# Attention and a two-layer feed-forward block on one core: three pairs of feature tiles, DVE transposes placed behind the low parts, and a first chunk in a written order with its masks put into PSUM by TensorE

## The chip, the cores and the metric

The kernel runs on one core of a Trainium2 chip. The metric is device time in microseconds (us) of one execution, lower is better; the value that counts is the median of the runs shown. Engines are called TensorE (PE, with its weight loads PEld), VectorE (DVE), ScalarE (ACT), GpSimd (POOL) and SyncE (SP, which issues most DMAs).

## The reference

Eight batches, eight heads, 576 positions, head size 64. Heads 0 to 3 see the last 32 positions, heads 4 to 7 see every 32nd position up to their own. Then comes a feed-forward block with a squared ReLU.

```python
def _attn_ref(q, k, v):
    scores = scale * np.matmul(q, k.transpose(0, 1, 3, 2))
    rel = pos[:, None] - pos[None, :]
    mask_local = (rel >= 0) & (rel < stride)                       # stride = 32, heads 0..3
    mask_strided = (rel >= 0) & (pos[None, :] % stride == pos[:, None] % stride)   # heads 4..7
    scores = np.where(masks[None], scores, -1000000000.0)
    attn = np.exp(scores - np.max(scores, axis=-1, keepdims=True))
    attn = attn / (np.sum(attn, axis=-1, keepdims=True) + 1e-09)
    return np.matmul(attn, v)
...
x = attn_out.transpose(0, 2, 1, 3).reshape(B * S, H * D)           # 4608 x 512
h = np.maximum(x @ w_in, 0.0)                                      # w_in 512 x 2048
return (h * h) @ w_out                                             # w_out 2048 x 512
```

## The kernel before

The 4608 tokens are cut into nine chunks of 512 (`NCHUNK`). A chunk is 16 rows of 32 positions (`RUNS` lists from which batches; a run is a stretch of rows of one batch). For each chunk the attention output is made as a transposed tile x, in two halves: `"l"` for the local heads and `"s"` for the strided heads. Each half stands as a high part (`xlh`, `xsh`, a rounded float32r copy) and a low part (`xll`, `xsl`, the rest), so that three float32r products (high x high, high x low, low x high) stand for one float32 product.

The feed-forward block has 16 feature tiles of 128. `up(c, j)` makes tile j of chunk c with 12 products of 512 columns in a PSUM bank (bank j % 2). ACT then takes relu and square and casts the result to `gh` (L411 to L413; in chunk 0 ACT and DVE share this, L408 and L409), and DVE subtracts to get the low part `gl` (L414), which reads the bank of `up` for the last time. `gh` and `gl` come from `gpool` with two buffers each. `down(c, js)` adds tile by tile into four PSUM banks of y, 12 products for a tile (L429), two tiles at a time from chunk 1 on. The order on TensorE from chunk 1 on is: up j, up j+1, down j-2 and j-1, up j+2, and so on.

The attention of chunk c+1 is worked in beside chunk c. `local(c)` is a generator: loads; scores (L232) and mask add (L184); maximum, subtraction and exponential; sum and division; 16 transposes of 32 x 256 on DVE (L263), four at a step; outputs (L278) with copy and low part of x (L285, L286). `take` runs the next step where `plan` or, for chunk 0, `plan0` says, behind the last TensorE instruction. `strided(c)` is a generator too: GpSimd multiplies (L353, L375) and DVE reduces (L354, L376), with loads `qs`, `ks`, `vs` from a pool `s3` of five slots, and ends with x written by ACT and GpSimd (L387, L388). `xpool` has two buffers, so the x of chunk c+1 can be written when chunk c-1 has been used.

The weights come as raw 64-bit numbers. `convert()` makes a high and a low float32 part of each of the 16 weight blocks, in two pieces of 512 columns: ACT scales the raw block (L128) and makes `z` (L143), DVE joins `z` to the word (L146), ACT or DVE makes the high part (L150, L152), GpSimd the low part (L153). In the start `z` stands in PSUM banks 0 and 1, the same as those of `up`. `behind` lets these steps follow an instruction of the last `up`.

Chunk 0 starts with 60 products of zeros, the local scores and, in `strided0()`, the strided scores of rows 0 to 7 of two batches, done by TensorE with 32 x 32 blocks: 128 float32 products, which show as 256 instructions (L322).

Within a program the framework places each engine's instructions in an order that a planner works out ahead of time from estimated durations, earlier traced instructions first; `issue_after(i)` sets an edge on `i`'s own engine: what is traced under it stands behind `i` there. On the chip each engine works through its list in order.

Of the kernel before, what the change touches and what calls it, by code (L numbers as in the profile page):

```python
# [18 lines left out]
STR = 32  # L19
# [3 lines left out]
P = 128  # L23
# [20 lines left out]
NWARM = 60  # L44
NEARLY = 3
# [23 lines left out]
def attn_moe(ctx: ExitStack, tc, qk_d, v_d, qk_p, v_p, q_s, k_s, v_s, w_in, w_out, masks, consts, out):  # L69
# [5 lines left out]
    gpool = pool("gpool", 2)  # L75
# [17 lines left out]
    warm = const.tile([P, P // 2], F32, name="warm")  # L93
    nc.gpsimd.memset(warm, 0.0)
    zero = warm.bitcast(BF16)

    last = {}
# [6 lines left out]
    zhome, zturn = (0, 1), iter(range(1000))  # L104

    def fetch(k):

        p, which = order[k]
        src = (w_out if which else w_in)[p].bitcast(U32).rearrange("p (n t) -> p n t", t=2)
        if k < 12:  # L110
            raw = wpool.tile([P, 1024, 2], U32, name=f"raw{k}", tag=f"w{k + 8 if k < 8 else k + 4}")
            nc.sync.dma_start(out=raw, in_=src)
            raws[k] = [(raw, slice(0, 1024))]
        else:
            raws[k] = []
            for i in range(0, 1024, WP):
                raw = spool.tile([P, WP, 2], U32, name=f"raw{k}_{i}", tag="s3", bufs=5)
                nc.sync.dma_start(out=raw, in_=src[:, i : i + WP])
                raws[k].append((raw, slice(i, i + WP)))

    def convert():

        split = None

        def scale(k):
            for raw, _ in raws[k]:

                nc.scalar.activation(f32(raw[:, :, 1]), f32(raw[:, :, 1]), AF.Prelu, scale=2.0**-112, alpha=-(2.0**32))  # L128

        scale(0)  # L130
        for k in range(NFT):
            p, which = order[k]
            t = wpool.tile([P, 2, 1024], F32R, name=f"w{which}_{p}", tag=f"w{k}")
            (wo if which else wi)[p] = t[:, 0], t[:, 1]
            cuts = [(raw[:, i : i + WP], sl.start + i) for raw, sl in raws.pop(k) for i in range(0, sl.stop - sl.start, WP)]
            for raw, at in cuts:

                if zhome is None:
                    z = ypool.tile([P, WP], F32, name=f"z{k}_{at}", tag="ysb").bitcast(U32)
                else:  # L140
                    z = psum(zhome[next(zturn) % len(zhome)], f"z{k}_{at}").bitcast(U32)
                w, hi, lo = raw[:, :, 1], t[:, 0, at : at + WP], t[:, 1, at : at + WP]
                first_step = nc.scalar.activation(z, raw[:, :, 0], AF.Copy, bias=-0.49, scale=2.0**-29 * (1 - 2.0**-9))  # L143
                if split:
                    split()
                last["v"] = nc.vector.scalar_tensor_tensor(out=w, in0=w, scalar=3, in1=z, op0=ALU.logical_shift_left, op1=ALU.bitwise_or)  # L146

                def split(w=w, hi=hi, lo=lo, at=at, k=k):
                    if k == 0 or at:
                        last["v"] = nc.vector.tensor_copy(hi, f32(w))  # L150
                    else:
                        last["a"] = nc.scalar.copy(hi, f32(w))  # L152
                    last["g"] = nc.gpsimd.tensor_sub(lo, f32(w), f32(hi))  # L153
                    if at and 4 <= k < 12:
                        fetch(k + 4)

                if k == 0 and at:
                    split()
                    split = None
                if not at and k + 1 < NFT and k + 1 in raws:  # L160
                    with tc.issue_after(first_step.ins):
                        scale(k + 1)
                yield
        split()
# [12 lines left out]
    def softmax(u, s, e, mask, n, first):  # L177

        sv = [t[:, : 8 * n].rearrange("p (g w k) -> p g w k", g=2, w=4) for t in s]
        mx = small.tile([P, 16], F32, name=f"mx{u}", tag="lmx")  # L180
        sm = small.tile([P, 16], F32, name=f"sm{u}", tag="lsm")
        halves = [slice(8 * h, 8 * (h + 1)) for h in range(2)]
        for h, sl in enumerate(halves):
            nc.vector.tensor_tensor(out=e[:, sl].rearrange("p (g w) k -> p g w k", g=2), in0=sv[h], in1=mask, op=ALU.add)  # L184
        yield
        wide = lambda t, sl: t[:, sl].unsqueeze(2).broadcast_to([P, 8, n])
        if first:
            parts = halves
        else:
            parts = [slice(0, 16)]  # L190
            wide = lambda t, sl: t.unsqueeze(2).broadcast_to([P, 16, n])
        for sl in parts:
            nc.vector.tensor_reduce(out=mx[:, sl], in_=e[:, sl], op=ALU.max, axis=AX.X)
        for h, sl in enumerate(parts):
            eng = nc.vector if first and not h else nc.gpsimd
            eng.tensor_sub(e[:, sl], e[:, sl], wide(mx, sl))
        for h, sl in enumerate(parts):
            last["a"] = nc.scalar.activation(e[:, sl], e[:, sl], AF.Exp, scale=SCALE)
            last[f"exp{h}"] = last["a"]
        yield  # L200
        for h, sl in enumerate(parts):
            nc.vector.tensor_reduce(out=sm[:, sl], in_=e[:, sl], op=ALU.add, axis=AX.X)
            nc.vector.tensor_scalar_add(sm[:, sl], sm[:, sl], 1e-9)
            nc.vector.reciprocal(sm[:, sl], sm[:, sl])
            if first and h:
                last["g"] = nc.gpsimd.tensor_mul(e[:, sl], e[:, sl], wide(sm, sl))
            else:
                last["v"] = nc.vector.tensor_mul(e[:, sl], e[:, sl], wide(sm, sl))
        yield

    def local(c):

        first = c == 0
# [6 lines left out]
        mk = mpool.tile([P, 4, 2 * STR], F32, name=f"mk{c}", tag="mk")  # L220
        (nc.scalar if first else nc.sync).dma_start(out=mk, in_=masks[c])
        yield
        rows = rows_of(c)
        s = [psum(3 + h, f"s{c}_{h}") for h in range(2)]
        for w in range(4):
            for pr in range(2):
                for b in range(4):
                    r = 4 * w + b
                    k0 = TC + rows[r][2]
                    for h in range(2):  # L230
                        hd = slice(D * h, D * (h + 1))
                        last["mm"] = nc.tensor.matmul(  # L232
                            s[h][STR * b : STR * (b + 1), (4 * pr + w) * 64 : (4 * pr + w + 1) * 64],
                            qk[pr][hd, STR * r : STR * (r + 1)], qk[pr][hd, k0 : k0 + 64], start=True, stop=True,
                        )
        e = lpool.tile([P, 16, 2 * STR], F32, name=f"e{c}", tag="e")
        yield from softmax(f"{c}", s, e, mk.unsqueeze(1).broadcast_to([P, 2, 4, 2 * STR]), 2 * STR, first)
        if first:
            vt = wpool.tile([P, 2, 1024], F32, name="v0", tag="w6")
# [437 lines left out]
```

## Time and profile before

| | us |
|---|---|
| median of 3 runs | 967.02 |
| lowest, highest | 966.3, 973.57 |
| the profiled execution, in all | 965.91 |
| its span, first to last instruction | 964.1 |
| TensorE busy (matmul) in the span | 871.2 |
| DVE, ACT, GpSimd busy | 544.0, 331.0, 511.3 |
| mean granted TensorE clock | 0.95 of full speed |

A profiled execution is read on its own time: the span is its length from the first to the last instruction, and 1.8 us of the measured time lie around it. A granted clock of 1.00 is TensorE at 2.4 GHz, 0.5 is 1.2 GHz, and a mean between them is a mix in time. "Releaser" is the instruction whose end let a waiting one go; "issue" is idle time for which the profile shows no cause.

### The profile page before, as it was taken

The numbers are of one execution on the slowest core, as the hardware profiler recorded it, in microseconds if no ns is written. First come the engines' busy times: TensorE is split into PE (matmuls) and PEld (weight loads), VectorE is DVE, ScalarE is ACT, GpSimd is POOL, SyncE is SP. The second block draws the span as 40 slices with busy tenths as digits, with TensorE's granted clock in tenths as the row PEclk, the third lists the DMA queues.
The fourth block names the chain that finished last, engine by engine and source line by source line (L and its number), as shares of the span: only waits on it lengthen the run. The fifth ranks groups of instructions, "written<-read, shape, count | busy, mean of one in ns | idle before, by whom it ended". The sixth has DMA issues, their size and how long they took to land. (4 is left out here: it accounts for less than half of the span.)

```text
span 964.1 us, 15516 instructions
## 1 busy us (share of the span) xinstructions
PE 871.2 (90%) x6252; PEld 710.8 (74%) x6252; DVE 544.0 (56%) x1047; ACT 331.0 (34%) x574; POOL 511.3 (53%) x532
## 2 busy tenths in 40 slices
PE   5399888997999989997989897998889998999997
PEld 5377667786878777786778785876678886888886
DVE  4498867765686558755776567554866152111111
ACT  3365643332333233332323232332223332333332
POOL 2484477486767868558768494767767100000000
PEclk9599899999999989998989998998989999999999
DMA  9625143222120222022300430121300120001001
GB/s 379 283 96 184 36 137 121 85 85 96 51 71 30 97 67 94 0 66 94 114 28 1 134 115 11 41 82 64 113 1 1 48 88 1 1 1 44 0 1 44
DMA packets 23096, 72.39 MB, mean 75 GB/s; under 512 B 2544, under 2 KB 4848, under 8 KB 21488
## 3 DMA queue, kind: packets, MB, share of 16 engines
q1 hardware_dynamic: 22592, 71.05, 21.2%
q8 instruction: 49, 0.80, 0.3%
q10 hardware_dynamic: 432, 0.34, 0.1%
q14 instruction: 23, 0.19, 0.1%
HBM read 61.95 MB, written 9.44 MB: 74 GB/s over the span
## 5 line engine op out<-in xcount | busy, mean ns | idle before, releaser
L429 PE MATMUL y<-w,gh 128*128 128x512 f32 x1152 | 354.9, 390 | 0.0
L402 PE MATMUL h<-xlh,w 128*128 128x512 f32 x576 | 217.8, 420 | 67.9 <-DVE gl L414 61.2
L353 POOL TENSOR_TENSOR pq<-ks,qs 128x512 f32<-128x512 f32 (+2 forms) x224 | 216.5, 994 | 81.8 <-DMA ks<-k_s 44.4
L375 POOL TENSOR_TENSOR pp<-vs,sc 128x320 f32<-128x320 f32 (+11 forms) x224 | 208.5, 967 | 95.6 <-issue 65.9
L429 PEld LDWEIGHTS y<-w,gh 128*128 128x128 f32 x1152 | 216.5, 188 | 45.2
L429 PE MATMUL y<-w,gl 128*128 128x512 f32 x576 | 223.2, 389 | 0.0
L402 PE MATMUL h<-xsh,w 128*128 128x512 f32 x576 | 208.7, 404 | 0.0
L414 DVE TENSOR_TENSOR gl<-h,gh 128x512 fp32r<-128x512 f32 x144 | 98.9, 686 | 175.8 <-ACT gh L413 174.7
L402 PEld LDWEIGHTS h<-xlh,w 128*128 128x128 f32 x576 | 115.3, 200 | 104.3 <-DVE gl L414 72.9
L354 DVE TENSOR_REDUCE sc<-pq 128x8 f32<-128x512 f32 (+2 forms) x224 | 116.0, 534 | 108.7 <-POOL pq L353 107.3
L411 ACT ACTIVATE h<-h 128x512 f32<-128x512 f32 x128 | 74.5, 582 | 290.5 <-PE h L402 286.3
L413 ACT CAST gh<-h 128x512 fp32r<-128x512 f32 x144 | 84.5, 588 | 210.9 <-PE y L429 190.4
L376 DVE TENSOR_REDUCE qs<-pp 128x64 f32<-128x64 f32 (+12 forms) x224 | 117.9, 533 | 62.4 <-POOL pp L375 61.3
L402 PEld LDWEIGHTS h<-xsh,w 128*128 128x128 f32 x576 | 114.1, 198 | 25.2
L429 PEld LDWEIGHTS y<-w,gl 128*128 128x128 f32 x576 | 108.1, 188 | 22.6
L402 PE MATMUL h<-xll,w 128*128 128x512 f32 x288 | 118.4, 412 | 0.0
L402 PE MATMUL h<-xsl,w 128*128 128x512 f32 x288 | 116.0, 404 | 0.0
L412 ACT ACTIVATE h<-h 128x512 f32<-128x512 f32 x128 | 74.5, 582 | 3.7
L402 PEld LDWEIGHTS h<-xsl,w 128*128 128x128 f32 x288 | 57.1, 198 | 12.7
L402 PEld LDWEIGHTS h<-xll,w 128*128 128x128 f32 x288 | 57.8, 201 | 10.9
L153 POOL TENSOR_TENSOR w<-raw,w 128x512 fp32r<-128x512 f32 x32 | 44.9, 1407 | 36.5 <-ACT w L152 19.5
L263 DVE STREAM_TRANSPOSE pt<-e 32x256 f32<-32x256 f32 x128 | 55.7, 435 | 1.8
(67 smaller groups left out, 429.8 us busy)
## 6 DMA issues: line engine op xcount, KB each, us to landing
vs<-v_s SPq DMA_DIRECT2D x18, 576.0 KB, 4.3
y<-ysb SPq DMA_DIRECT2D x35, 256.0 KB, 2.6
v<-v_d SPq DMA_DIRECT2D x16, 512.0 KB, 4.9
qk<-qk_d SPq DMA_DIRECT2D x14, 544.0 KB, 5.1
raw<-w_in SPq DMA_DIRECT2D x7, 1024.0 KB, 11.2
raw<-w_out SPq DMA_DIRECT2D x5, 1024.0 KB, 13.3
ks<-k_s SPq DMA_DIRECT2D x8, 576.0 KB, 4.3
raw<-w_out SPq DMA_DIRECT2D x6, 512.0 KB, 5.3
```

The costliest lines, as they stand in the source:

```text
L153: last["g"] = nc.gpsimd.tensor_sub(lo, f32(w), f32(hi))
L263: nc.vector.transpose(out=pt[to : to + STR, :, STR * b : STR * (b + 1)], in_=e5[STR * b : STR * (b + 1), :, a, STR * half : STR * (half + 1)],
L353: nc.gpsimd.tensor_mul(pv, kt[:, a : a + m, :], qt[:, i - i0 : i - i0 + 1, :].broadcast_to([P, m, D]))
L354: nc.vector.tensor_reduce(out=sc[:, i - i0, a : a + m], in_=pv, op=ALU.add, axis=AX.X)
L375: nc.gpsimd.tensor_mul(pv, vt[:, a : a + nd, :n], sc[:, il : il + 1, :n].broadcast_to([P, nd, n]))
L376: nc.vector.tensor_reduce(out=ot[:, il, a : a + nd], in_=pv, op=ALU.add, axis=AX.X)
L402: done = nc.tensor.matmul(ph, wi[p][a][:, wsl], x["ls"[kt // 2], b][:, kt % 2, :], start=n == 0, stop=n == 11)
L411: nc.scalar.activation(ph, ph, AF.Relu)
L412: nc.scalar.activation(ph, ph, AF.Square)
L413: last["gh"] = nc.scalar.copy(gh, ph)
L414: nc.vector.tensor_sub(gl, ph, f32(gh))
L429: done = nc.tensor.matmul(y_ps[c][t], gg[:, sl], w[:, wsl], start=j == 0 and k == 0, stop=j == NFT - 1 and k == 2)
```

## The change

- `gpool` gets three buffers instead of two: three pairs of `gh` and `gl`.
- `take` places the steps of `local` also behind the last low part `gl` on DVE, the transposes in groups of four to a step among them.
- `up` sorts its 12 products by half and part of x, and becomes a generator that pauses after the fourth product. In chunk 0 the first four tiles use banks 0, 1, 3 and 4.
- The strided part gets two slots for queries of its own (`sq`) and three slots (`s3`) for keys and values instead of five for all; in chunks 1 to 3 keys and values come in one load (`kv_s`). In chunk 0 the strided steps of chunk 1 stand behind the last `gl` on DVE and the last weight step on GpSimd.
- Chunk 0 up to its second `up` is a function `begin()`, whose instructions keep the written order on each engine (`in_order`). The masks go into PSUM by products of the identity with the mask, and the scores are added to them; maximum and subtraction read PSUM. The strided weights are put into zero-padded 128 x 128 blocks, so that the strided outputs are 32 products of 128 columns (before: 128 of 32). Fetches of raw weights 1 to 3 are made to wait for instructions of other engines. Only the first weight piece has its `z` in PSUM.
- The raw weights 12 to 14 also come whole, and only the last one in two pieces through `s3`.

The diff, cut to its core:

```diff
-    gpool = pool("gpool", 2)
+    gpool = pool("gpool", 3)
...
+    @contextmanager
+    def in_order():
+        traced = nc.cur_bb.bb.instructions
+        n = len(traced)
+        yield
+        for i in traced[n:]:
+            if i.engine in ends:
+                tc.add_manual_dep(i, ends[i.engine].name, mybir.DependencyInfo(mybir.DependencyClass.NoSync, mybir.DependencyReason.DATA), reason="in order")
+            ends[i.engine] = i
+
+    def wait(ins, after):
+        tc.add_manual_dep(ins.ins, after.ins.name, mybir.DependencyInfo(mybir.DependencyClass.Sync, mybir.DependencyReason.DATA), reason="gate")
...
-        if k < 12:
-            raw = wpool.tile([P, 1024, 2], U32, name=f"raw{k}", tag=f"w{k + 8 if k < 8 else k + 4}")
+        if k < 15:
+            raw = wpool.tile([P, 1024, 2], U32, name=f"raw{k}", tag=f"w{RAW[k]}")
...
+    def piece(k, raw, at, t, home=None):
+        z = psum(home, f"z{k}_{at}") if home is not None else ypool.tile([P, WP], F32, name=f"z{k}_{at}", tag="ysb")
...
+    def begin():
+        zero = lpool.tile([P, 256], F32, name="zero", tag="e")
+        nc.vector.memset(zero, 0.0)
...
+        zeros(12)
+        qk = loads(0)
...
+        fetch(0)
...
+        for h in range(2):
+            for pr in range(2):
+                nc.tensor.matmul(s[h][:, 256 * pr : 256 * (pr + 1)], ident, mk.rearrange("p w k -> p (w k)"), start=pr == 0, stop=False, skip_group_check=True)
+        scores(0, qk, s, False)
+        ss = [ybank(f"ss{h}") for h in range(2)]
+        for h in range(2):
+            nc.tensor.matmul(ss[h][:, :256].rearrange("p (n k) -> p n k", k=STR), ident, mask_s.unsqueeze(1).broadcast_to([P, 8, STR]), start=True, stop=False, skip_group_check=True)
...
+        scale(0)
+        ka, kb = (piece(*c, home=h) for c, h in zip(cuts(0), (0, None)))
+        next(ka)
+        for h in range(2):
+            top = nc.vector.tensor_reduce(out=st["mx"][:, half[h]], in_=sv[h], op=ALU.max, axis=AX.X)
+        for h in range(2):
+            nc.vector.tensor_sub(el[:, half[h]], sv[h], wide(st["mx"][:, half[h]], 2 * STR))
+            nc.scalar.activation(el[:, half[h]], el[:, half[h]], AF.Exp, scale=SCALE)
+        wait(fetch(1), top)
...
+        wait(fetch(2), nc.scalar.activation(es, es, AF.Exp, scale=SCALE))
...
+        wait(zeros(14), top)
...
+        pts = wpool.tile([P, 16, P], F32, name="pts0", tag="w5")
+        nc.gpsimd.memset(pts, 0.0)
+        x = x_tiles(0)
+        o = [psum(3 + a, f"o0_{a}") for a in range(2)]
+        outputs([vt[:, pr] for pr in range(2)], pt, o)
+        xs = [by_parity(x, o, a) for a in range(2)]
+        for src, (xh, _) in xs:
+            done = nc.scalar.copy(xh, src)
+        nc.vector.tensor_mul(es, es, wide(st["sms"], STR))
+        for b in range(4):
+            blk = slice(STR * b, STR * (b + 1))
+            nc.vector.transpose(out=pts[blk, :, blk], in_=es[blk])
...
+        ups = [up(0, j) for j in range(2)]
+        for u in ups:
+            next(u)
+        wait(fetch(3), done)
+        for k in range(4, 8):
+            last["f"] = fetch(k)
...
-                    for b in range(4):
-                        ks = slice(STR * b, STR * (b + 1))
-                        last["mm"] = nc.tensor.matmul(
-                            o[b][STR * hd : STR * (hd + 1), (a * 4 + w) * STR : (a * 4 + w + 1) * STR],
-                            v4[ks, n, STR * a : STR * (a + 1)], pts[ks, n], start=True, stop=True,
-                        )
...
+                    nc.tensor.matmul(o[a][STR * hd : STR * (hd + 1), P * w : P * (w + 1)], v4[:, n, STR * a : STR * (a + 1)], pts[:, n], start=True, stop=True)
...
-            qt = spool.tile([P, MI, D], F32, name=f"qs{u}", tag="s3", bufs=5)
-            kt = spool.tile([P, NI, D], F32, name=f"ks{u}", tag="s3", bufs=5)
-            vt = spool.tile([P, D, NI], F32, name=f"vs{u}", tag="s3", bufs=5)
+            qt = spool.tile([P, MI, D], F32, name=f"qs{u}", tag="sq", bufs=2)
             nc.sync.dma_start(out=qt[:, :ni], in_=q_s[b, :, i0:i1])
+            if i1 == S0:
+                kv = spool.tile([P, 2, S0 * D], F32, name=f"kv{u}", tag="s3", bufs=3)
+                nc.sync.dma_start(out=kv, in_=kv_s[b])
...
+            else:
+                kt = spool.tile([P, NI, D], F32, name=f"ks{u}", tag="s3", bufs=3)
+                vt = spool.tile([P, D, NI], F32, name=f"vs{u}", tag="s3", bufs=3)
...
-        ph = psum(j % 2, f"h{c}_{j}")
-        prods = [(kt, a, b) for kt in range(4) for a, b in ((0, "h"), (0, "l"), (1, "h"))]
-        if c == 0 and j < 2:
-            prods.sort(key=lambda t: (t[1], t[0] // 2, t[2]))
+        ph = psum((0, 1, 3, 4)[j] if c == 0 and j < 4 else j % 2, f"h{c}_{j}")
+        prods = [(k, a, b) for k in range(4) for a, b in ((0, "h"), (1, "h"), (0, "l"))]
+        prods.sort(key=lambda t: (t[0] // 2, t[2]) if c else (t[0] // 2, t[2], t[1]))
...
-                    for i in (last["pe"], *(weights_end.values() if c == 2 else ())):
+                    for i in (last["pe"], last["gl"], *(weights_end.values() if c == 2 else ())):
...
-                if c == 1:
-                    st = behind(weights_end, st)
+                if c < 2:
+                    st = behind(weights_end if c else {"v": last["gl"], "g": last["g"]}, st)
...
+    for s in range(NS + 2):
+        with tc.issue_after(last["f"].ins):
+            slot(s)
```

## Rows read from the trace of the kernel before

**Rows 1.** Stretches: us, busy PE, PEld, DVE, ACT, POOL, mean granted clock, DMA, GB/s.

```profile
0.00:55.00 55.00, 29.14 (x773) 25.80 (x774) 28.25 (x58) 18.18 (x30) 21.64 (x29) 0.72 0.72 291
55.00:150.00 95.00, 84.80 (x591) 68.39 (x590) 79.30 (x123) 53.57 (x89) 58.29 (x52) 0.95 0.39 127
150.00:866.00 716.00, 664.78 (x4483) 540.41 (x4483) 421.65 (x846) 228.60 (x404) 431.34 (x453) 0.96 0.18 59
866.00:964.00 98.00, 92.47 (x408) 76.22 (x407) 14.76 (x22) 30.61 (x53) 0.00 (x0) 1.00 0.06 22
```

**Rows 2.** Waits of TensorE, whole span: who for whom, us, times, longest.

```profile
PE h L402 <- DVE gl L414: 61.2, 22, 5.8
PE os L322 <- issue: 8.4, 2, 4.4
```

**Rows 3.** The same waits, from 150 to 866 us.

```profile
PE h L402 <- DVE gl L414: 51.0, 18, 5.8
```

**Rows 4.** Chain of waits near the end: start, length, what.

```profile
847.44 2.00 PE o L278 x128
...
882.31 5.44 PE y L429 x24
887.75 5.44 PE h L402 x24
```

**Rows 5.** Timeline of TensorE at the scores taken in chunk 7.

```profile
780.43 1.48 PE L232 MATMUL s<-qk 64*32 64x64 f32 x128
```

**Rows 6.** Timeline of ACT and DVE in the last chunk: square, cast, low part.

```profile
880.24 0.58 ACT L412 ACTIVATE h<-h 128x512 f32<-128x512 f32 x1
...
884.84 0.59 ACT L413 CAST gh<-h 128x512 fp32r<-128x512 f32 x1 [1.30 <-PE y L429]
885.46 0.69 DVE L414 TENSOR_TENSOR gl<-h,gh 128x512 fp32r<-128x512 f32 x1 [7.42 <-ACT gh L413]
```

**Rows 7.** Timeline around the wait for the low part of tile 12, chunk 1.

```profile
231.14 1.57 POOL L353 TENSOR_TENSOR pq<-ks,qs 128x512 f32<-128x512 f32 x2 [3.50 <-DMA ks<-k_s]
...
231.77 0.59 ACT L413 CAST gh<-h 128x512 fp32r<-128x512 f32 x1 [1.65 <-PE y L429]
...
238.68 1.10 DVE L354 TENSOR_REDUCE sc<-pq 128x8 f32<-128x512 f32 x2 [1.11 <-POOL pq L353]
239.70 0.68 DVE L414 TENSOR_TENSOR gl<-h,gh 128x512 fp32r<-128x512 f32 x1
240.44 0.79 PE L402 MATMUL h<-xlh,w 128*128 128x512 f32 x1 [5.75 <-DVE gl L414]
```

**Rows 8.** Timeline around a wait for the low part of tile 3, chunk 4.

```profile
481.86 6.71 DVE L263 STREAM_TRANSPOSE pt<-e 32x256 f32<-32x256 f32 x15
488.61 0.69 DVE L414 TENSOR_TENSOR gl<-h,gh 128x512 fp32r<-128x512 f32 x1
489.35 0.80 PE L402 MATMUL h<-xlh,w 128*128 128x512 f32 x1 [2.75 <-DVE gl L414]
```

**Rows 9.** Timeline of GpSimd: first steps of the strided parts of chunks 5 and 8.

```profile
322.86 0.16 POOL L345 MEMSET sc<- 128x72 f32 x1
...
639.39 0.19 POOL L345 MEMSET sc<- 128x108 f32 x1
```

**Rows 10.** Timeline of TensorE in the start of chunk 0.

```profile
24.62 3.66 PE L278 MATMUL o<-pt,v 64*64 64x32 f32 x124 [0.81 <-DVE pt L255]
...
33.65 1.54 PE L322 MATMUL os<-tmp_s 32*32 32x32 f32 x128 [4.03 <-issue]
...
46.43 1.22 PE L402 MATMUL h<-xlh,w 128*128 128x512 f32 x2 [6.50 <-DVE raw L146]
```

**Rows 11.** Groups of DVE by line, 0 to 46 us: busy, mean ns, idle before.

```profile
L146 DVE SCALAR_TENSOR_TENSOR raw<-raw,z 128x512 uint32<-128x512 uint32 x5 | 3.4, 681 | 0.4 <-ACT z L143 0.4
```

**Rows 12.** The same, 55 to 150 us.

```profile
L146 DVE SCALAR_TENSOR_TENSOR raw<-raw,z 128x512 uint32<-128x512 uint32 x26 | 26.5, 1030 | 6.1 <-ACT z L143 5.9
```

**Rows 13.** DMA issues of the page: count, KB each, median us to landing.

```profile
vs<-v_s SPq DMA_DIRECT2D x18, 576.0 KB, 4.3
```

More of the change, by code (lines that the diff above doesn't have):

```diff
@@ L121, in convert @@
-    def convert():
[L123 to L159, printed above, removed]
@@ new lines, in scale, with cuts @@
+    def scale(k):
+        for raw, _ in raws[k]:
+            nc.scalar.activation(f32(raw[:, :, 1]), f32(raw[:, :, 1]), AF.Prelu, scale=2.0**-112, alpha=-(2.0**32))
+    def cuts(k):
+        p, which = order[k]
+        t = wpool.tile([P, 2, 1024], F32R, name=f"w{which}_{p}", tag=f"w{HOME[k]}")
+        (wo if which else wi)[p] = t[:, 0], t[:, 1]
+        return [(k, raw[:, i : i + WP], sl.start + i, t) for raw, sl in raws.pop(k) for i in range(0, sl.stop - sl.start, WP)]
+    def convert():
+        before = None
+        for k in range(3, NFT):
+            for k, raw, at, t in cuts(k):
+                g = piece(k, raw, at, t)
+                step = next(g)
+                if before:
+                    run(before)
+                    if at == 0 and k - 1 in NEXT:
+                        fetch(NEXT[k - 1])
+                next(g)
+                before = g
@@ L160, in convert @@
                 if not at and k + 1 < NFT and k + 1 in raws:
-                    with tc.issue_after(first_step.ins):
+                    with tc.issue_after(step.ins):
                         scale(k + 1)
                 yield
-        split()
+        run(before)
     xt = {}
@@ L214, in local, with loads @@
+    def loads(c):
         nk = STR * (CR + len(RUNS[c]))
@@ L219, in local, with scores @@
             qk.append(t)
-        mk = mpool.tile([P, 4, 2 * STR], F32, name=f"mk{c}", tag="mk")
-        (nc.scalar if first else nc.sync).dma_start(out=mk, in_=masks[c])
-        yield
+        return qk
+    def scores(c, qk, s, start):
         rows = rows_of(c)
-        s = [psum(3 + h, f"s{c}_{h}") for h in range(2)]
         for w in range(4):
@@ L316, in strided0 @@
+        next(ka)
+        next(kb)
+        scale(2)
+        v4 = vs.rearrange("p (n d) -> p n d", d=D)
+        o = [ybank(f"os{a}") for a in range(2)]
         for a in range(2):
@@ L523, in attn_moe @@
-    next(st)
-    for k in range(NEARLY, 8):
-        fetch(k)
-    with tc.issue_after(last["pe"].ins):
-        last["pe"] = zeros(0, 40, exp_l)
-    with tc.issue_after(last["pe"].ins):
-        next(lo)
-    next(st)
-    for _ in range(2):
-        next(ungated)
-    chain(lo)
-    chain(st)
-    weights = behind({"a": last["a"]}, ungated)
-    for _ in range(2 * NEARLY - 2):
-        next(weights)
-    zhome = None
+    plan0 = (2, 4, 6, 7, 8, 9, 10, 11, 13)
+    with in_order():
+        done, ups = begin()
@@ L540, in attn_moe, with slot @@
+    for u in ups:
+        run(u)
+    ungated = convert()
+    weights_end = st = cost = ds = None
+    weights = behind({"a": last["a"], "v": last["v"]}, ungated)
     NS = NCHUNK * NFT
-    for s in range(NS + 2):
+    def slot(s):
+        nonlocal weights, weights_end, st, cost, ds
         c, j = divmod(s, NFT)
         if s < NFT:
-            with tc.issue_after(last["pe"].ins):
-                last["pe"] = up(c, j)
             if s >= 2:
                 with tc.issue_after(last["pe"].ins):
+                    *_, last["pe"] = up(c, j)
+                with tc.issue_after(last["pe"].ins):
```

320 lines of the change are left out of this document (165 added, 155 removed).

## The prediction

> **What bounds the kernel now.** I read the busy table by stage first [rows 1]: TensorE is the engine to serve (664.8 of 716 us busy in chunks 1 to 7, 92.5 of 98 in the last), while VectorE (DVE) and GpSimd stand at 59 and 60% in chunks 1 to 7. TensorE's waits then say what it lacks: 61.2 us on the low parts `gl` in 22 places and 8.4 us of "issue" in the strided outputs of chunk 0 [rows 2], and 6.5 us once on a weight step [rows 10]. Of the 61.2, 51.0 lie in chunks 1 to 7 [rows 3].
>
> How far is that from a floor? In the chain of waits, where nothing disturbs it, 24 up products take 5.44 us, 24 down products as long, and the outputs of a chunk 2.00 [rows 4]; the scores take 1.48 [rows 5]. A chunk has 16 up and 16 down tiles of 12 products, so 16 x 5.44 + 2.00 + 1.48 = 90.5 us. Seven are 633.7, and they took 716: 82.3 over. 51.0 of it is waiting. The other 31 is matmuls at half clock after the waits: the mean grant there is 0.96, and 1.00 in the last chunk, which has no such waits [rows 1]. So a wait costs its length and some 60% more.
>
> Why is `gl` late? In the undisturbed last chunk [rows 4, 6] the square ends at 880.82, but the cast `gh` starts at 884.84, released by a down product: with two pairs of feature tiles it needs the pair of two tiles back, which "down" still reads. `gl` ends at 886.15, and the up products that need its bank start at 887.75. The slack is some 1.5 us; DVE work put ahead of `gl` that runs longer is paid by TensorE. Two things do that. For tile 12 of a chunk, `gl` starts at 239.70 though its cast ended at 232.36: reduces stand before it, paced by GpSimd, which was itself 3.5 us late on a load, and TensorE waits 5.75 us [rows 7]. There are five such waits (chunks 1 to 5), 22 us together. For tiles 2 to 4, fifteen transposes of 6.71 us in a row stand ahead of a `gl`: 2.75 us [rows 8]. There are twelve of these, 26 us.
>
> **Third pair.** The first cast of two tiles no longer waits for "down": 884.84 becomes 880.9, 4.0 us sooner; the second can start where the first starts now, 2.8 sooner [rows 6]. Slack goes from 1.5 to 5.5 and 4.3 us. For the five waits at tile 12 I expect the first `gl` to go ahead of the reduces and the second to take its old place, needed half a pair of tiles (2.72 us) later: of 5.8, 4.7, 5.2, 2.5 and 4.0 there remain 3.1, 2.0, 2.5, 0 and 1.3, 9 of 22 us. Bounds: 0 if DVE's order mends by itself, 22 if the wait just goes to the other tile.
>
> **Transposes behind gl.** The 16 transposes (7.2 us a chunk by rows 8) go in two lots of eight (3.5 us) behind the low parts of tiles 9 and 11. Such a lot fits between two pairs of low parts, 10.9 us apart, so the 26 us go. What is late next: the last lot must end before the outputs, which stand one down pair and one up pair (10.9 us) behind tile 11. Its `gl` takes 4.0 of that, the transposes 3.5; 3.4 us are left, and reduces can use them up. Cost 0 to 3.5 us a chunk; I take 1 (7 in all), since DVE is two fifths idle [rows 1]. With 6 us of half clock after the waits that stay, 9 + 7 + 6 = 22 of the 82.3 remain; ends 5 and 60.
>
> **Order of the 12 products; merged loads; three load slots.** The products are as many as before: 0. With three slots instead of five (queries have two of their own), a run's values wait until an older tile is free. GpSimd today runs far ahead: it begins chunk 5's strided part at 322.9 and chunk 8's at 639.4 [rows 9], while chunk 8 starts on TensorE at 866. That is 316.5/3 = 105.5 us a chunk, more than the 90.5 floor, so the lead shrinks; but chunk 8's part ends at about 745, and I expect chunk 8 on TensorE at 144 + 656 = 800. Cost 0, margin 55 us. On SP, the fetches of weights 1, 2 and 3 now wait for a reduce, an exponential and a cast of other engines; behind the third stand weights 4 to 7 and every later load, the next chunk's queries and the strided tiles among them. At 576 KB in 4.3 us [rows 13] a weight of 1 MB needs 8 us, and weight 3 is wanted a pair of slots (10.9 us) after the first ups: 0, or up to 5 us of chunk 0 if that cover is gone.
>
> **First chunk, start.** Today the local outputs end at 28.3; the strided outputs, 256 small instructions with two waits for nothing the profile shows, end at 39.9; then the first up waits 6.5 us for a bank in which a weight's `z` stands, and starts at 46.4 [rows 10], at half clock (mean grant 0.72 to 55, rows 1). Two ups are done at 55. After: 64 instructions of four times the columns. Per 32 columns the rows give 12 ns (1.54/128) and 30 ns (3.66/124), so 64 x 48 to 118 ns = 3.1 to 7.6 us, and 15 at half clock; I take 7. The `z` of later pieces leaves PSUM, so the 6.5 go. Eight of the two tiles' 24 up products run earlier; the other 16 take 3.6 us, or 7.2 at half clock, say 5. With 3 us (1 to 4) for the zero-padded transposes and the copies: 28 + 3 + 7 + 5 = 43, ends 36 and 53. The masks on TensorE are 12 instructions of 256 columns, 1.2 to 2.8 us by the same rows, and take four adds from DVE: 0 net, from -2 to +3.
>
> **First chunk, rest.** That gain of 12 us is not all kept. From 55 to 150 TensorE needs 14 ups and 16 downs, 30 x 2.72 + 3.5 = 85 us, and DVE was busy 79.3 of 95 [rows 1]. DVE now also gets the first strided run of chunk 1, which ran beside the old start and now queues behind `gl` (I estimate 8 us), and two weight pieces fewer are done by then (3 us): 90 us. At 83% as today that is 108 us, at 95% it is 95. So chunk 1 starts at 138 to 151; I take 144 (150 today), with ends 128 (TensorE alone) and 158.
>
> DVE's weight step on [128 x 512] takes 681 ns in the start [rows 11] and 1030 ns from 55 to 150 [rows 12], when GpSimd is at work. The Trainium skill, SBUF — State Buffer, section "Who interferes with whom", says that a VectorE instruction with two SBUF inputs and a GpSimd instruction that reads SBUF block each other. The trace agrees with 0.35 us a step; by that rule the strided run that is pushed among the weights would lengthen the 26 steps that remain by up to 9 us where they run free today, which lies within the end of 158; I take nothing, since their mean shows that they collide already.
>
> **Sum.** Profiled execution: span 964.1, 965.9 in all (1.8 outside), 1.1 under the median of 967.0. After: 1.8 + 144 + 633.7 + 22 + 98.1 (last chunk and tail, as now) = 900 us.
>
> **Rivals.**
> - *Waits move.* GpSimd's pace stays in DVE's queue, the second `gl` and the outputs take over the waits. For: DVE's reduces follow GpSimd around tile 12 [rows 7]. Against: without a late load or transposes, `gl` is on time. 50 of the 82 stay, chunk 1 at 147: 1.8 + 147 + 633.7 + 50 + 98.1 = 931.
> - *Floor.* Only 5 us stay, chunk 1 at 130: 869.
> - *The third pair does nothing,* because the cast is held by something else (ACT's order, the bank): the 82 stay, chunk 1 at 144 to 150: 960 to 966. Against: the release by a down product [rows 6].
> - *Slower: the strided part loses its lead.* With three slots a run's tiles cannot land until the run before is written out, and that waits for TensorE to be done with a chunk. If each run shows two loads of 4.3 us [rows 13], 2.5 runs a chunk make 105.5 + 21.5 = 127 us for each of chunks 4 to 7 instead of about 93. Chunk 8 then starts at 144 + 3 x 93 + 4 x 127 = 931, and the total is 1031. It decides once the strided part is some 55 us later than I count. Against: a slot comes free when a run's values are used, and the next run's keys need only one.
>
> **How the numbers follow.** Forecast (880 to 920) 0.53, waits move (920 to 957) 0.25, floor (under 880) 0.08, no effect (957 to 977) 0.08, slower 0.06. One per cent is about what a measurement of this kernel can tell from no change. Faster by over 1%: 0.53 + 0.25 + 0.08 = 0.86. The range 868 to 950 leaves out about 0.04 below and 0.16 above.
>
> **What would show it.** Waits of up on `gl` in chunks 1 to 7 near 10 us, none for tiles 2 to 4; the first of two casts released by the square; a mean grant there above 0.98; transposes in lots of eight behind `gl`; first two ups done by 36 to 53, chunk 1 at 138 to 151; GpSimd's last strided step before 800. I am wrong if outputs wait on transposes, if up waits on strided x tiles, or if chunk 0 grows.

## The result and the profile after

The changed kernel takes 902.13 us in the median of four runs (900.78 to 902.53), the kernel before 966.66 beside it: a ratio of 0.932, interval 0.927 to 0.936, so 6 to 7% faster. The forecast was 900, from 868 to 950. Its profiled execution took 901.9 us with a span of 900.1.

Busy time by stage of the changed kernel, with the columns of [rows 1] (the stages now end where its own chunks start):

```profile
0.00:40.00 40.00, 30.53 (x524) 20.04 (x525) 20.70 (x34) 15.90 (x23) 8.48 (x10) 0.87 0.76 298
40.00:135.00 95.00, 83.67 (x593) 66.76 (x591) 83.11 (x140) 55.89 (x90) 69.90 (x63) 0.98 0.43 158
135.00:803.00 668.00, 649.48 (x4479) 532.96 (x4480) 424.37 (x852) 230.61 (x405) 434.97 (x459) 0.98 0.19 62
803.00:900.00 97.00, 92.93 (x410) 76.61 (x409) 14.17 (x21) 30.16 (x52) 0.00 (x0) 0.99 0.06 22
```

Chunks 1 to 7 go from 716 to 668 us, the rest of the gain is ahead of them: chunk 1 starts at 135.0 instead of 150.3. The work of DVE and GpSimd there is the same (424 and 435 us; 422 and 431 before). What shrank is TensorE's idle time, from 51.2 to 18.5 us, and its busy time over the floor of 633.7, from 31.1 to 15.8. Not all of the latter is half clock: summed over the stretches with a granted clock of 0.50, TensorE was busy there for 45 us before and 23 us now, and half of that is lost, 23 and 11 us.

Waits of TensorE in the changed kernel, whole span, which answer to [rows 2]:

```profile
PE h L499 <- DVE gl L513: 26.5, 12, 6.9
PE os L405 <- issue: 2.4, 1, 2.4
PE h L499 <- ACT xsh L484: 1.8, 1, 1.8
```

The same from 135 to 803 us, which answers to [rows 3]; 4.5 us of it lie ahead of chunk 1's first product:

```profile
PE h L499 <- DVE gl L513: 21.3, 9, 6.9
```

ACT and DVE in its last chunk, cast and low part of tiles 12 and 13 with the square of the first, and the up products that need their banks, which answer to [rows 6]:

```profile
872.10 0.58 ACT L511 ACTIVATE h<-h 128x512 f32<-128x512 f32 x1
872.72 0.59 ACT L512 CAST gh<-h 128x512 fp32r<-128x512 f32 x1
873.34 0.69 DVE L513 TENSOR_TENSOR gl<-h,gh 128x512 fp32r<-128x512 f32 x1 [6.15 <-ACT gh L512]
...
876.76 0.59 ACT L512 CAST gh<-h 128x512 fp32r<-128x512 f32 x1 [1.35 <-PE y L528]
877.38 0.69 DVE L513 TENSOR_TENSOR gl<-h,gh 128x512 fp32r<-128x512 f32 x1 [3.35 <-ACT gh L512]
...
879.45 1.07 PE L499 MATMUL h<-xlh,w 128*128 128x512 f32 x4
...
882.17 1.07 PE L499 MATMUL h<-xlh,w 128*128 128x512 f32 x4
```

The first cast of a pair follows its square at once; the second is still released by a down product. Where nothing disturbs them, as here, the low parts end 5.4 and 4.1 us before the up products that need their banks (1.6 before).

The transposes stand behind the low parts in lots of eight, as DVE's timeline in chunk 5 shows, which answers to [rows 8]:

```profile
575.36 0.68 DVE L513 TENSOR_TENSOR gl<-h,gh 128x512 fp32r<-128x512 f32 x1
575.95 3.57 DVE L229 STREAM_TRANSPOSE pt<-e 32x256 f32<-32x256 f32 x8
```

And the largest wait left, also in chunk 5, which answers to [rows 7]: TensorE, ACT, DVE and GpSimd around the low part of tile 13.

```profile
591.56 2.07 PE L277 MATMUL o<-pt,v 64*64 64x32 f32 x128
...
596.44 0.59 ACT L512 CAST gh<-h 128x512 fp32r<-128x512 f32 x1 [1.71 <-PE y L528]
...
600.08 1.57 POOL L450 TENSOR_TENSOR pq<-ks,qs 128x512 f32<-128x512 f32 x2 [3.12 <-DMA ks<-k_s]
601.40 0.81 DVE L451 TENSOR_REDUCE sc<-pq 128x8 f32<-128x512 f32 x2 [3.41 <-POOL pq L450]
...
607.59 0.69 DVE L451 TENSOR_REDUCE sc<-pq 128x8 f32<-128x512 f32 x1 [1.12 <-POOL pq L450]
608.19 0.68 DVE L513 TENSOR_TENSOR gl<-h,gh 128x512 fp32r<-128x512 f32 x1
...
608.93 1.65 PE L499 MATMUL h<-xlh,w 128*128 128x512 f32 x3 [6.91 <-DVE gl L513]
```

Up of tile 13 had ended at 591.63. Its cast came 4.8 us later, released by the down products that stand behind the 2 us of outputs. In DVE's list seven reduces of the next run of the strided part stand ahead of the low part. DVE stood idle for 3.4 us before the first of them, since GpSimd waited 3.1 us for its keys, and then followed GpSimd's pace. So the low part started 11 us after its cast had ended. Each of chunks 1 to 6 has a wait at this place (3.56, 0.70, 1.99, 0.91, 6.91, 1.04: 15.1 us). In chunk 3 the cast itself is late, 11 us after its up, with the strided part's exponential ahead of it on ACT.

TensorE in the start, which answers to [rows 10]:

```profile
7.50 3.65 PE L317 MATMUL s<-mk,fixed 128*128 128x256 f32 x8 [2.11 <-DMA fixed<-consts]
11.08 1.48 PE L262 MATMUL s<-qk 64*32 64x64 f32 x128
...
27.12 2.11 PE L499 MATMUL h<-xlh,w 128*128 128x512 f32 x8 [1.16 <-ACT xlh L382]
31.59 3.52 PE L405 MATMUL os<-pts,tmp 128*32 128x128 f32 x64 [2.35 <-issue]
```

The first two ups are done at 39.8 us (54.9 before).

### The profile page after: what moved, and what is told of

Read it like the earlier page. It is cut to its first block, busy times and chain, and to the rows that moved or that the text cites. A ratio compares the mean times of both kernels' runs of the same rounds, so it can differ in the third digit from the quotient of the medians.

```text
span 900.1 us, 14986 instructions
## 1 busy us (share of the span) xinstructions
PE 856.6 (95%) x6002; PEld 696.4 (77%) x6002; DVE 542.3 (60%) x1045; ACT 332.5 (37%) x570; POOL 513.3 (57%) x530
## 4 chain that ended last, share of the span: by engine, by line
PE 40%; POOL 9%; DVE 6%; issue 3%; DMA 1%; ACT 0%; POOLq 0%; ACTq 0%
PE y L528 20%; PE h L499 19%; POOL pp L472 5%; POOL pq L450 4%; DVE pt L229 3%; DVE sc L451 1%; DVE gl L513 1%; DMA ks<-k_s 1%; PE s L262 0%; DVE qs L473 0%; POOL xsl L485 0%; DMA y<-ysb 0%; PE o L277 0%; ACT gh L512 0%; DVE e L216 0%
## 5 line engine op out<-in xcount | busy, mean ns | idle before, releaser
L472 POOL TENSOR_TENSOR pp<-vs,sc 128x320 f32<-128x320 f32 (+11 forms) x176 | 168.5, 994 | 67.8 <-issue 36.5
L450 POOL TENSOR_TENSOR pq<-ks,qs 128x512 f32<-128x512 f32 (+7 forms) x176 | 179.2, 1045 | 44.6 <-DVE sc L451 31.4
L499 PE MATMUL h<-xlh,w 128*128 128x512 f32 x576 | 160.7, 402 | 29.2 <-DVE gl L513 26.5
L499 PE MATMUL h<-xsh,w 128*128 128x512 f32 x576 | 158.7, 398 | 2.1 <-ACT xsh L484 1.8
L499 PEld LDWEIGHTS h<-xlh,w 128*128 128x128 f32 x576 | 108.2, 191 | 57.4 <-DVE gl L513 32.0
L499 PEld LDWEIGHTS h<-xsh,w 128*128 128x128 f32 x576 | 110.6, 192 | 26.7 <-ACT xsh L484 2.5
L499 PE MATMUL h<-xsl,w 128*128 128x512 f32 x288 | 90.8, 397 | 0.0
L499 PE MATMUL h<-xll,w 128*128 128x512 f32 x288 | 90.7, 397 | 0.0
L499 PEld LDWEIGHTS h<-xll,w 128*128 128x128 f32 x288 | 55.3, 192 | 12.2 <-issue 0.3
```

Source lines behind the costliest of these rows:

```text
L450: nc.gpsimd.tensor_mul(pv, kt[:, a : a + m, :], qt[:, i - i0 : i - i0 + 1, :].broadcast_to([P, m, D]))
L472: nc.gpsimd.tensor_mul(pv, vt[:, a : a + nd, :n], sc[:, il : il + 1, :n].broadcast_to([P, nd, n]))
L499: done = nc.tensor.matmul(ph, wi[p][a][:, wsl], x["ls"[k // 2], b][:, k % 2, :], start=n == 0, stop=n == 11)
```

## The experiments

All ratios are to the kernel before on the same chip. First a measure of what counts as a difference.

**The changed kernel again.**

> The changed kernel as it is, beside the other kernels on one chip, as a measure of what a difference of some us means: 900 to 905 us.

899.66 us, ratio 0.930 (0.928 to 0.932). The waits of chunks 1 to 7 are the same to within 0.2 us; chunk 1 starts 1.5 us earlier. Two sets of runs of one kernel differ by 2.5 us; less than 4 us decides nothing below.

**Transposes not behind gl.**

```diff
-                    for i in (last["pe"], last["gl"], *(weights_end.values() if c == 2 else ())):
+                    for i in (last["pe"], *(weights_end.values() if c == 2 else ())):
```

> The changed kernel, with the steps of the local part placed only behind the last TensorE instruction again, not behind the last low part. Three pairs stay. Theory of the recorded sum (each edit ends its own waits): the third pair leaves the waits for tiles 2 to 4 alone, so 26 us of waiting and some 60% more in half clock come back, 902 + 42 = 944 us. Rival (what counts is the slack of gl alone): before, the transposes of 6.7 us with a slack of 1.5 us made waits of 2.2 us on average; with the slack of 5.4 and 4.1 us that the third pair gave, nearly nothing is left of them: 900 to 908 us, and the placement is cover without work of its own.

913.91 us, 0.945 (0.943 to 0.946): 12 us, outside both ranges, nearer to the rival's 0 to 6 than to my sum's 42. The slack swallows most of it, but not all: a row of up to 16 transposes and the reduces beside it take longer than the slack of 5.4 us. The waits of up on the low parts of tiles 2 to 4 in chunks 1 to 6 come to 10.4 us (1.6 in the changed kernel), those on tile 13 to 11.3 (15.1). DVE and TensorE at tiles 4 to 6 of chunk 5:

```profile
558.20 7.17 DVE L229 STREAM_TRANSPOSE pt<-e 32x256 f32<-32x256 f32 x16
565.40 1.08 DVE L451 TENSOR_REDUCE sc<-pq 128x5 f32<-128x320 f32 x2
566.39 1.28 DVE L513 TENSOR_TENSOR gl<-h,gh 128x512 fp32r<-128x512 f32 x2
...
567.13 1.80 PE L499 MATMUL h<-xlh,w 128*128 128x512 f32 x4 [3.11 <-DVE gl L513]
```

**Two pairs.**

```diff
-    gpool = pool("gpool", 3)
+    gpool = pool("gpool", 2)
```

> The changed kernel with two pairs of feature tiles again; everything else stays. Theory of the recorded sum: slack back to 1.5 us, and the five waits at tile 12 stand at 22 us again in place of the 15 us that the second of the pair has now; the transposes do nothing, since they stand behind gl: about 7 us more waiting and 60% of it in half clock, 913 us (908 to 918). Rival (slack alone counts): every piece of DVE work ahead of a gl, reduces above all, is paid at 3 to 4 us less slack, 30 us or more: 930 to 945 us.

920.07 us, 0.950 (0.948 to 0.951): 18 us, between the two ranges. Chunks 1 to 6 wait 3.2 to 5.4 us each ahead of tile 14 (in chunk 2 nearly all of it ahead of tile 15): the low part of the pair's first tile takes the old place again. Chunk 3:

```profile
411.05 0.59 ACT L512 CAST gh<-h 128x512 fp32r<-128x512 f32 x1 [1.65 <-PE y L528]
413.36 1.55 POOL L450 TENSOR_TENSOR pq<-ks,qs 128x512 f32<-128x512 f32 x2 [2.86 <-DMA ks<-k_s]
...
417.95 0.68 DVE L513 TENSOR_TENSOR gl<-h,gh 128x512 fp32r<-128x512 f32 x1
418.68 2.08 PE L499 MATMUL h<-xlh,w 128*128 128x512 f32 x4 [4.72 <-DVE gl L513]
```

**Both undone.** The two edits together.

> The changed kernel with two pairs and with the local steps behind the last TensorE instruction only: what is left of the change is the new first chunk, the order of products, the merged loads and the slots. Theory: chunks 1 to 7 are as before the change (716 us in place of 668), chunk 1 starts at about 135 us: 902 + 48 = 950 us (943 to 957), waits on gl near 55 us. Rival (the loads, the slots or the order have a part in the gain of chunks 1 to 7): 915 to 940 us. Rival (the new slots cost something that the third pair hides): over 957 us.

956.75 us, 0.988 (0.986 to 0.989), at the upper end of the theory's range. Busy time of chunks 1 to 7 and waits of TensorE there:

```profile
133.80:856.50 722.70, 670.39 (x4480) 545.65 (x4481) 426.98 (x855) 230.19 (x404) 440.13 (x462) 0.95 0.18 57
```

```profile
PE h L499 <- DVE gl L513: 49.9, 16, 5.5
PE h L499 <- ACT xsh L484: 5.6, 1, 5.6
```

So all of the change but these two edits is worth 12 us of the 65 to 68: in the traces chunk 1 starts 16.5 us earlier, and chunks 1 to 7 take 7 us more. From there, the third pair alone takes 43 us off (956.8 to 913.9), the placement alone 37 (to 920.1), both 55. Their single gains sum to 80 us, so 25 us of them are the same gain counted twice.

**Five shared slots.** On top of both undone, the tiles of queries, keys and values share five slots.

```diff
-            qt = spool.tile([P, MI, D], F32, name=f"qs{u}", tag="sq", bufs=2)
+            qt = spool.tile([P, MI, D], F32, name=f"qs{u}", tag="s3", bufs=5)
```

(and five for each tile of `s3`)

> The kernel with two pairs and local steps behind TensorE only (956.8 us), with five slots shared by queries, keys and values as before the change, in place of two and three. It asks why chunks 1 to 7 took 723 us there where the kernel before took 716. Theory of the recorded sum (slots and merged loads cost nothing): no change, 953 to 960 us. Rival (three slots make loads land late and cost the 7 us): chunks 1 to 7 at 714 to 718 us, 947 to 952 us.

953.69 us, 0.983 (0.981 to 0.986): no change beyond the 4 us. Chunks 1 to 7 take 720.7. The number of slots costs nothing that shows. Why these chunks take some 5 to 7 us more than in the kernel before stays open; with both undone it is TensorE's busy time that grew, by 5.6 of the 7 us, and its idle time by 1.1; one wait of 5.6 us, for the strided half of x, is new in it.

**The old order of products** from chunk 1 on.

```diff
-        prods = [(k, a, b) for k in range(4) for a, b in ((0, "h"), (1, "h"), (0, "l"))]
-        prods.sort(key=lambda t: (t[0] // 2, t[2]) if c else (t[0] // 2, t[2], t[1]))
+        prods = [(k, a, b) for k in range(4) for a, b in ((0, "h"), (0, "l"), (1, "h"))]
+        if c == 0:
+            prods.sort(key=lambda t: (t[0] // 2, t[2], t[1]))
```

> The changed kernel with the old order of the 12 up products (high x high, high x low, low x high in turn) from chunk 1 on; chunk 0 keeps halves apart. Theory of the recorded sum: as many products of the same size, 902 us, within 3 us. Rival (the new order does something: the first products no longer want the low part of x, or the strided half comes later): the old order makes the start of each chunk wait for x, 1 to 2 us a chunk, 908 to 916 us.

898.9 us, 0.927 (0.924 to 0.929): the order from chunk 1 on is worth nothing, as counted.

**Late outputs.** They are taken behind the down pair of step 6.

```diff
-    plan = {..., 6: (0, 1, 0)}
+    plan = {..., 6: (0, 0, 1)}
```

> The changed kernel with the outputs of the local part taken behind the pair of down tiles of step 6 and no longer between the pair of up tiles and it. The computation stays. Theory (the wait moved to the second gl of the pair, whose cast is released by the down products): the down pair comes 2.0 us earlier, so the cast of tile 13 does, and the waits ahead of tile 15 (15.6 us in chunks 1 to 6) become shorter by up to 2 us each, 8 us and 60% more in half clock: 890 to 897 us. Rival (the wait is made by reduces that follow GpSimd and stand ahead of that gl on DVE; the cast is long done): no change, 899 to 905 us, with the waits at the same place.

887.84 us, 0.917 (0.916 to 0.918): 12 to 14 us faster than the changed kernel, a little more than the theory's range. DVE and GpSimd at the place in chunk 5 shown above:

```profile
588.49 0.69 DVE L513 TENSOR_TENSOR gl<-h,gh 128x512 fp32r<-128x512 f32 x1
...
594.20 1.58 POOL L450 TENSOR_TENSOR pq<-ks,qs 128x512 f32<-128x512 f32 x2 [3.28 <-DMA ks<-k_s]
595.53 0.69 DVE L451 TENSOR_REDUCE sc<-pq 128x8 f32<-128x512 f32 x1 [3.58 <-POOL pq L450]
```

GpSimd waits for its keys as long as ever. But the cast of tile 13 comes 2.6 us after its up, not 4.8, and its low part now stands ahead of the reduces that this load delays. It is the place in DVE's list that counts: in chunks 1, 2, 4, 5 and 6 of the changed kernel the low part starts 4.4 to 11 us after its cast has ended, so a cast that comes 2.2 us sooner changes nothing there with the list as it is. Counted in the two traces, 2 to 11 reduces fewer stand ahead of the low part of tile 13 in each of chunks 1 to 6 (10 in chunk 5). So the theory is near in size, but the earlier cast is not by itself what took the waits away. Why the planner placed the low part earlier is not shown. No wait ahead of tile 15 is left; 6.6 us turn up at tiles 0 and 1 of the next chunks.

**Four pairs.** To make room, the strided queries get one slot and y two buffers.

```diff
-    gpool = pool("gpool", 3)
+    gpool = pool("gpool", 4)
```

> The changed kernel with four pairs of feature tiles; to make room, the strided queries have one slot in place of two and the tiles of y two buffers in place of three. Theory (with three pairs the cast of tile 13 needs the pair of tile 10, which the down products behind the outputs still read; its low part then falls behind reduces that wait for GpSimd): with a fourth pair no cast waits for down, the cast of the second tile starts 1.3 us after its up like that of the first, the waits ahead of tile 15 go, and the time comes near that of the kernel with late outputs: 885 to 893 us. Rival (late outputs helped by where they put DVE's work, not by the cast): 898 to 906 us. Against both: one slot of queries makes the strided part late, and chunks 4 to 7 wait for it: over 910 us.

918.3 us, 0.947 (0.945 to 0.950): the last of the three. The cast itself did as the first theory says, in chunk 1 for both tiles of the pair (12 and 13):

```profile
211.18 0.59 ACT L512 CAST gh<-h 128x512 fp32r<-128x512 f32 x1
...
213.90 0.59 ACT L512 CAST gh<-h 128x512 fp32r<-128x512 f32 x1
```

Both follow their squares, and no wait ahead of tile 15 is left. But GpSimd now waits for queries:

```profile
POOL pq L450 <- DMA qs<-q_s: 54.1, 13, 8.0
```

and the reduces that it delays hold the low part of tile 14 (up to 14 us after its cast), with waits of 7.7, 7.7, 2.8 and 8.4 us ahead of tile 0 of chunks 2, 4, 5 and 6. A fourth pair without that price was not tried, so whether the cast alone would bring the gain of the late outputs stays open.

**Two pairs and late outputs.**

> The changed kernel with late outputs and with two pairs of feature tiles. Theory (with two pairs every cast waits for down, and the outputs ahead of down delay the cast of tile 12 by their 2 us as they do that of tile 13 with three): the waits ahead of tile 14, 26 us in chunks 1 to 6 with two pairs, become shorter by some 2 us each and 60% more in half clock, 898 to 906 us, and the third pair is worth 10 to 18 us beside late outputs as it is without them (18). Rival (late outputs need the slack of the third pair to do anything): 915 to 921 us.

903.95 us, 0.934 (0.932 to 0.936): late outputs take 16 us off with two pairs, 12 to 14 with three. The third pair is worth 16 us beside late outputs and 18 without them: these two add up.

**No edge on the strided steps of chunk 1.**

```diff
-                if c < 2:
-                    st = behind(weights_end if c else {"v": last["gl"], "g": last["g"]}, st)
+                if c == 1:
+                    st = behind(weights_end, st)
```

> The changed kernel without the edge that puts the strided steps of chunk 1 behind the last low part on DVE and the last weight step on GpSimd in chunk 0. Theory of the recorded sum (the strided run that the edge pushes among the weights is paid by DVE, which bounds chunk 0): without the edge it runs beside the start, DVE has some 3 to 8 us less to do behind 40 us, and chunk 1 starts at 128 to 133 us in place of 135: 894 to 900 us. Rival (the steps then stand ahead of weight steps and of the softmax in the start, and the first two ups end later by as much): chunk 1 at 134 to 140 us, 901 to 908 us.

890.99 us, 0.919 (0.917 to 0.921): 9 to 11 us off, 3 us below the theory's range, and the way is another. Chunk 1 starts at 133.5, which is no difference to the 133.4 and 135.0 of the changed kernel. GpSimd's first strided product is at 53.3 us instead of 62.7, and the part is done at 132 instead of 141, so chunk 1 no longer waits for the strided half of x (1.8 us), and chunks 1 to 3 take 99.8, 91.1 and 90.9 us (103.0, 91.9 and 95.7). With the lead of 9 us DVE's list has other reduces ahead of the low parts of tiles 12 to 15 in chunks 1 to 3, and the same as in the changed kernel in chunks 4 to 6. In chunk 3 the wait ahead of tile 15 is gone although the outputs stand where they did and the cast of tile 13 comes 4.8 us after its up.

**Both improvements.**

> The changed kernel with both edits that made it faster: outputs behind the down pair (887.8 us), and no edge on the strided steps of chunk 1 (891.0 us). Theory (they act in different places, the one ahead of tile 15 in chunks 1, 3 and 5, the other at the start of chunk 1): their gains of 14 and 11 us overlap only in chunks 1 and 3, 877 to 883 us. Rival (both only shift where DVE's steps stand, and the same waits are taken away by either): no better than the better one, 885 to 891 us.

882.0 us, 0.912 (0.910 to 0.913), the fastest kernel of the study: 18 to 20 us under the changed one. Chunks 1 to 7 and TensorE's waits in them:

```profile
135.00:783.90 648.90, 641.95 (x4481) 527.36 (x4482) 423.09 (x847) 227.92 (x404) 428.91 (x455) 1.00 0.19 63
```

```profile
PE h L499 <- DVE gl L513: 12.3, 8, 5.8
```

The 5.8 us lie ahead of chunk 1's first product. From there on 15 us over the floor of 633.7 are left: 7.0 of idle time, and 8.3 of busy time. The clock stands at half in one stretch alone:

```profile
135.00:140.60 5.60, 5.48 (x12) 3.79 (x12) 3.44 (x9) 0.59 (x1) 5.60 (x9) 0.50 0.49 170
```

That is a loss of 2.7 us; the other 5.5 are not half clock.

**Masks added by DVE.** In `begin()`, the mask products are replaced by four additions in PSUM.

```diff
-                nc.tensor.matmul(s[h][:, 256 * pr : 256 * (pr + 1)], ident, mk..., start=pr == 0, stop=False, ...)
-        scores(0, qk, s, False)
+        scores(0, qk, s, True)
+        for h in range(2):
+            t4 = s[h].rearrange("p (g w k) -> p g w k", g=2, w=4)
+            nc.vector.tensor_tensor(out=t4, in0=t4, in1=mk.unsqueeze(1).broadcast_to([P, 2, 4, 2 * STR]), op=ALU.add)
```

(and the same for the strided scores)

> The changed kernel with the masks of chunk 0 added by DVE into the PSUM banks of the scores, as four additions, and no longer put there by TensorE. It asks what that one edit of the start is worth. Theory of the recorded sum (0 net, from a gain of 2 us by the edit to a loss of 3): the 12 products of identity and mask (4.8 us by the changed kernel's trace) go, the scores start when their loads land, and four additions of some 0.4 to 0.7 us stand on DVE's path to the softmax: the first two ups end at 38 to 42 us (39.8 with the edit), 898 to 904 us. Rival (DVE's path sets the end of the start, TensorE waits for its loads anyway): the four additions are paid in full, the first two ups end at 42 us or later. Rival (the products also keep TensorE's clock up while it waits): the scores and the outputs that follow run at half clock, and the first ups end at 42 us or later with longer instructions.

898.84 us, 0.928 (0.926 to 0.931), no difference in the total. In the trace the start itself is shorter:

```profile
6.42 1.71 PE L262 MATMUL s<-qk 64*32 64x64 f32 x128
...
23.64 3.33 PE L499 MATMUL h<-xlh,w 128*128 128x512 f32 x8 [1.16 <-ACT xlh L382]
```

```profile
8.18 1.30 DVE L318 TENSOR_TENSOR s<-s,mk 128x512 f32<-128x512 f32 x2 [7.05 <-PE s L262]
```

The scores no longer stand behind products that wait for the constants, and start at 6.4 us (11.1, and 9.6 in the second trace of the changed kernel). The first two ups end at 34.9 (39.8 and 37.1, and 37.1 to 40.0 in all twelve traces that have the mask products), and chunk 1 starts at 130.6. Chunks 1 to 7 take 669.6 (668.3 and 667.7), so of 3 to 4 us at the start of chunk 1 some 1 to 3 are left in the total. Neither rival holds, nor do the theory's 38 to 42 us; this edit of the change costs the start 2 to 5 us.

## Why the prediction was right, step by step

**The sum** was 1.8 + 144 + 633.7 + 22 + 98.1 = 900. Measured: 1.8 + 135.0 + 633.7 + 34.6 + 96.8 = 901.9. Two terms were off by 9 and 12.6 us with opposite signs. That the total came within 2 us of the forecast is luck; its terms were right to within 13 us.

**Signs.** Up waits on `gl` in chunks 1 to 7 for 16.7 us without the wait ahead of chunk 1 (near 10 was said), for tiles 2 to 4 only 1.6 (none). The mean grant is 0.98, where above 0.98 was said, and chunk 1 starts at 135.0 (138 to 151). One sign of being wrong came, in small: up waits once for the strided half of x, 1.8 us, for which the sum has no term.

**Third pair.** Right: the slack of 5.5 and 4.3 us is 5.4 and 4.1, the release is by the square and by a down product, and the wait at tile 12 went to the second low part. Its size was off: I said 9 us, measured 15.1, and chunk 5 alone has 5.6 us more than I gave it (6.9 in place of 1.3). I took the second low part to stand where the first stood and to be needed 2.7 us later. In chunk 5 DVE's list has it behind seven reduces that wait for a late load. The late outputs show that these reduces are the wait: with them behind the low part it is gone, and the load is as late as before.

**Transposes behind gl.** The waits at tiles 2 to 4 fell from 26 to 1.6 us as said, but that the placement does this was only part of it. Undone, it costs 12 us, not 26 and half clock: the third pair alone covers most of the same waits. I priced each edit against the kernel before, as if the other were not there.

**Outputs.** I took 7 us for outputs that wait for transposes. There is none: the outputs of chunk 5 follow the ups at once (591.56). Where they stand costs all the same: taken behind the down pair, they leave the kernel 12 to 14 us faster.

**Half clock.** I took 6 us, and TensorE's busy time is 15.8 over the floor, beside 18.5 us of idle time. These are the stretches at half clock in chunks 1 to 7:

```profile
134.98:144.07 9.09, 7.31 (x16) 5.30 (x17) 4.53 (x10) 2.56 (x5) 6.37 (x9) 0.50 0.28 90
225.99:232.81 6.82, 5.83 (x14) 4.56 (x15) 4.72 (x10) 1.16 (x3) 5.72 (x6) 0.50 0.00 0
417.14:420.55 3.41, 3.41 (x10) 2.64 (x9) 0.24 (x1) 1.49 (x3) 0.53 (x1) 0.50 0.02 5
604.87:615.11 10.24, 6.18 (x15) 4.83 (x16) 5.61 (x14) 3.38 (x8) 3.66 (x6) 0.50 0.01 2
```

TensorE is busy in them for 22.7 us, so 11 are lost. Another 3 are the floor, which is too low: chunk 7, which has no wait, takes 90.9 us and not 90.5. The last 1 to 2 are not accounted for. In the kernel before I had laid all of the 31 us to half clock; by the same sum it is 23, so a wait there costs its length and 45% more, not 60. The half clock and the second low part are the terms that were too small.

**Order, loads, slots.** The order from chunk 1 on and the number of slots are worth nothing, as counted, by two experiments. The merged loads were not undone. GpSimd's steps that answer to [rows 9], and its last:

```profile
314.13 0.16 POOL L442 MEMSET sc<- 128x72 f32 x1
...
627.10 0.18 POOL L442 MEMSET sc<- 128x108 f32 x1
...
723.89 1.57 POOL L485 TENSOR_TENSOR xsl<-ks,xsh 128x640 fp32r<-128x640 f32 x1 [2.08 <-ACT xsh L484]
```

That is 104.3 us a chunk (105.5 predicted); the last part is ready at 725 us (745), chunk 8 starts on TensorE at 803 (800). The rival in which the strided part loses its lead is ruled out.

**Start.** Two ups at 43 was said, 39.8 and 37.1 measured. The strided outputs took 3.5 us (2.0 in the second trace) and a wait of 2.4 us ahead of them; I took 7. The wait of 6.5 us for a bank with a `z` is gone, as said. The masks I had at net 0, from -2 to +3; the trace has them at 2 to 5 us of loss. Their 12 products take 4.8 and 3.1 us, not 1.2 to 2.8, and wait 2 us for the constants. Of the other edits of the start none was undone by itself.

**Rest of chunk 0.** From there to chunk 1 I counted 101 us (90 of DVE work), and it took 95.2 with 83.1 busy. DVE's strided reduces from 40 to 135 us grew by 3 us (12.7 in place of 9.5 from 55 to 150 before), not by the 8 that I estimated, and the weight step was no slower (against [rows 12]):

```profile
L140 DVE SCALAR_TENSOR_TENSOR raw<-raw,z 128x512 uint32<-128x512 uint32 x27 | 24.9, 933 | 4.9 <-ACT z L138 4.0 <-issue 0.6
```

I had named up to 9 us that these steps could grow; the trace has 933 ns in place of 1030. Step by step, the 8 of them that no GpSimd instruction overlaps take 678 to 695 ns (11 of 675 to 695 before), and each of the 12 that take over 800 (14 before) overlaps one. So pushing more of GpSimd's work among them (it is busy 69.9 of the 95 us, 58.3 before) did not make more of them slow. The Trainium skill, SBUF — State Buffer, section "Who interferes with whom", has it that a VectorE instruction with two SBUF inputs contends with a GpSimd instruction that reads SBUF; the trace agrees as far as only overlapped steps are slow. My comparison with the 681 ns of [rows 11] does not show it: four of those five steps overlap GpSimd too and take 675 to 696 ns, with `z` in PSUM.

**Last chunk and tail** took 96.8 in place of 98.1; why was not pursued.

## What to carry to other kernels

An in-order engine that serves a bottleneck (DVE's low parts for TensorE) has a slack, and what stands ahead of it costs only what exceeds that slack. Two edits that widen it or empty it cover the same waits, so undo them one at a time and together before adding up their gains. Then look at what stands ahead of the serving step in its engine's list and what paces that (here reduces behind a late load of a third engine): moving one line, which changed that order, gave 12 to 14 us more.

## What the hardware showed that I had not expected

Half clock costs about half as much as the waits beside it: some 23 us beside 51.2 of idle time in chunks 1 to 7 before, 11 beside 18.5 after, 3 beside 7.0 in the fastest kernel, by the time that TensorE was busy at a grant of 0.50. The busy time over the floor (31.1, 15.8, 8.3) overstates it. In the changed kernel the four stretches at half clock go with the waits of 4.5 and 1.8, 3.6, 2.0 and 6.9 us, and the five waits of 0.5 to 1.1 us have none. The length alone does not decide it: in the kernel before one of 1.8 us (chunk 4) has such a stretch and one of 2.6 (chunk 1) has none.

And one instruction group of the start runs at either level from one execution of the same kernel to the next: the eight mask products took 3.65 us in one trace of the changed kernel and 1.97 in the other, at a granted clock of 0.52 and 1.00, the strided outputs 3.52 and 1.95, at 0.53 and 1.00.
